# Causal score blocks of 32 tokens in lanes of 32 TensorE columns

## The chip, the core and the metric

The kernel runs on one core of a Trainium2 chip. Its engines are PE (TensorE: matmuls, with PEld for the loads of the stationary operand), DVE (VectorE), ACT (ScalarE), POOL (GpSimd) and SP (SyncE, which issues most DMAs). Matmuls read from SBUF and write to PSUM; DVE and ACT read PSUM and write SBUF. The metric is the device time of one execution in microseconds.

## What is computed

A recurrent attention with a complex, per-channel decay, followed by a two-layer network with a leaky ReLU. There are 4 sequences (batch), 8 heads, 768 steps and 48 channels a head.

```python
mag = np.sqrt(a_re * a_re + a_im * a_im)
scale = np.minimum(mag, 0.999) / (mag + 1e-06)
a_re_n, a_im_n = (a_re * scale, a_im * scale)
for t in range(S):
    ar, ai = (a_re_n[:, :, t, :, None], a_im_n[:, :, t, :, None])
    new_re = ar * S_re - ai * S_im
    new_im = ar * S_im + ai * S_re
    kv = np.einsum('bhd,bhe->bhde', k[:, :, t], v[:, :, t])
    S_re, S_im = (new_re + kv, new_im)
    y[:, :, t] = np.einsum('bhd,bhde->bhe', q[:, :, t], S_re)
...
h = x @ w_in                      # x: 3072 x 384, w_in: 384 x 2048
g = np.maximum(0.01 * h, h)
return (g @ w_out).astype(np.float32)
```

## The kernel before

The 768 steps are cut into six chunks of 128 tokens. Two sequences of one chunk make one of twelve parts (n = 0 to 11); a part is prepared as a whole, and its two sequences (units; 24 in all) go through the attention one after the other.

**Preparation** (prep, L392 to L560), on DVE and ACT. Inside a chunk, the decays are multiplied up: first over R = 8 consecutive tokens (L443, L446), then over the J = 16 ends of such segments by doubling (the tile xs, L448 to L467), and the products of the segments before are spread again over all tokens (L473 copies xs into xt with ACT; L482 and L487 on DVE use it). q is multiplied by the product up to its token and k by the inverse; the real and the imaginary part stand one below the other as 96 rows. The results go to the tile qkt, with 128 columns for the tokens, in the order (r, j): token 8j + r stands in column 16r + j. Ten DMAs a part move qkt into t96 (named t in the profile), 96 rows, one block of 128 columns for each head's q and k (L549 to L557, mostly in SP's queue). There is one qkt and one t96.

**Attention** (attend, L577 to L659), for each unit. With t96 as operands PE makes: ptk, the transposes of k for the state update (L588, copied to kn by ACT; not for the last chunk); ps, for each group of four heads the 128x128 scores of k against q (L601), one full-width matmul a head, four to a bank of PSUM; px, the output (L626): the masked scores and the old state rst times v and q, in 32-column lanes. In px each matmul has 32 columns of the array, and four lanes q = 0 to 3 write the four blocks of 32 PSUM partitions; its matmuls are issued in turn over the lanes. DVE multiplies a bank of scores with the causal mask into asb (L605), ACT and DVE split px into a rounded part xh and a rest xl (L628, L631). pu (L639) is the update of the state, one matmul a head, which reads v and kn. All matmuls of the attention are fp32, and an fp32 matmul that is no transpose leaves two records in the profile.

**MoE** (moe, L661 to L716), for the 256 tokens of each part: L679 to L681 (ph), leaky ReLU on ACT and DVE (tg, L685, L686), again a rounded part and a rest (gh, gl: L687, L688), then L696, L697, L702 (po). These matmuls take the whole array; 288 of them belong to a part, 3456 in all.

**Order.** The tile framework schedules the instructions of each engine statically from priorities: attention before MoE before preparation (PRIO_ATT, PRIO_MOE, PRIO_PREP). PE and DVE thus get one fixed sequence in which pieces of attention stand among MoE and preparation work of other parts. ptk, ps, px and pu share a ring of three PSUM banks (pool psa, tag att, L261). v has one buffer, 448 columns a unit (VW: pairs of heads in 112 columns, in which px finds its 32 columns and pu its 48). At the start, DVE, ACT and POOL also convert the weights into rounded parts and rests (L378 to L388).

At the start the mask is made by one matmul of two POOL-made matrices and copied to a 128x128 tile (L285 to L298), and each of the four heads of a bank is multiplied with it:

```python
nc.vector.tensor_tensor(
    out=asb, in0=ps, in1=mask.unsqueeze(1).to_broadcast([P, 4, C]), op=ALU.mult
)
```

## Time and profile before

| | |
|---|---|
| median of 3 runs | 686.41 us (685.02 to 686.86) |
| the profiled execution | 686.39 us |
| its span in the profile | 684.3 us |
| instructions | 14080 |
| granted TensorE clock, mean | 0.99 |
| HBM read, written | 49.55 MB, 4.72 MB |

What lies around the span is 686.39 - 684.3 = 2.1 us. The lines of the profile are read thus: a group names the source line, the engine, the operation, the tiles written and read, their shapes and the count; then the busy time in us, the mean of one in ns, and the idle time of the engine just before them with what ended it. Two groups of the page, a DVE operation of the MoE and an ACT copy of the attention:

```profile
L686 DVE TENSOR_TENSOR tg<-ph,tg 128x512 f32<-128x512 f32 x96 | 65.8, 688 | 53.4 <-ACT tg L685 51.0
...
L593 ACT COPY kn<-ptk 128x384 f32<-128x384 f32 x40 | 19.0, 474 | 47.6 <-PE ptk L588 47.6
```

### The profile page before, as it was taken

What the parts mean: (1) busy time and instruction counts of PE and PEld (TensorE: products, weight loads), DVE (VectorE), ACT (ScalarE), POOL (GpSimd) and SP (SyncE); (2) the same over time, 40 slices, a digit from 0 to 9 for tenths busy, and PEclk for the clock granted to TensorE, in tenths of its full rate; (3) what the DMA queues carried; (4) which work ended last, traced back from release to release, by engine and by line L of the source; (5) the groups of instructions that cost most, each with busy time, mean ns of one, the idle gap of its engine ahead of it and who ended that gap; (6) DMA issues with size and microseconds to landing.
All of it is one profiled execution on the core that took longest, in us unless ns stands there. A gap on an engine that the chain in (4) does not pass through costs nothing.

```text
span 684.3 us, 14080 instructions
## 1 busy us (share of the span) xinstructions
PE 577.0 (84%) x5732; PEld 555.4 (81%) x5732; DVE 550.2 (80%) x915; ACT 364.8 (53%) x815; POOL 78.0 (11%) x75
## 2 busy tenths in 40 slices
PE   0000475899999999999999999999999998999996
PEld 0000365798999899899999999989999997999996
DVE  5999899999989799898989989989889885233331
ACT  6245256457457275473755727538366277583321
POOL 5645255450000000000000000000000000000000
PEclk9999999999999999999999999999999999899998
DMA  8231733630421703408034070251701748750000
GB/s 329 78 103 69 217 107 119 151 129 29 110 100 52 186 15 88 136 29 209 8 86 145 28 187 25 69 146 51 184 4 51 210 166 194 269 196 13 24 1 29
DMA packets 26232, 74.27 MB, mean 109 GB/s; under 512 B 3376, under 2 KB 9520, under 8 KB 26160
## 3 DMA queue, kind: packets, MB, share of 16 engines
q1 hardware_dynamic: 25552, 71.71, 35.1%
q10 hardware_dynamic: 608, 1.59, 1.0%
q8 instruction: 47, 0.77, 0.5%
q14 instruction: 25, 0.20, 0.1%
HBM read 49.55 MB, written 4.72 MB: 79 GB/s over the span
## 4 chain that ended last, share of the span: by engine, by line
PE 45%; DVE 29%; DMA 12%; ACT 5%; issue 4%; SPq 2%; POOL 1%; ACTq 0%; DVEq 0%; POOLq 0%
DMA t<-qkt 6%; PE po L696 6%; PE po L697 6%; PE po L702 5%; DMA wck<-in_w_dram 5%; PE ph L679 5%; PE ph L680 5%; PE ph L681 5%; PE px L626 4%; PE ps L601 4%; PE pu L639 3%; DVE tg L686 2%; DVE tmp L443 2%; DVE wcv L378 2%; DVE gl L688 2%
## 5 line engine op out<-in xcount | busy, mean ns | idle before, releaser
L679 PE MATMUL ph<-xh,win_hi 128*128 128x256 f32 x576 | 165.2, 287 | 6.7 <-DVE tg L686 5.2
L680 PE MATMUL ph<-xl,win_hi 128*128 128x256 f32 x576 | 164.6, 286 | 2.7 <-DVE xl L631 2.7
L681 PE MATMUL ph<-xh,win_lo 128*128 128x256 f32 x576 | 164.0, 285 | 0.0
L696 PE MATMUL po<-gh,wout_hi 128*128 128x256 f32 x576 | 145.6, 287 | 0.5 <-ACT gh L687 0.5
L697 PE MATMUL po<-gh,wout_lo 128*128 128x256 f32 x576 | 144.8, 286 | 0.0
L679 PEld LDWEIGHTS ph<-xh,win_hi 128*128 128x128 f32 x576 | 110.0, 191 | 8.5 <-DVE tg L686 6.5
L680 PEld LDWEIGHTS ph<-xl,win_hi 128*128 128x128 f32 x576 | 110.1, 191 | 3.5 <-DVE xl L631 2.9
L696 PEld LDWEIGHTS po<-gh,wout_hi 128*128 128x128 f32 x576 | 110.3, 192 | 1.8 <-ACT gh L687 1.0
L697 PEld LDWEIGHTS po<-gh,wout_lo 128*128 128x128 f32 x576 | 110.5, 192 | 0.2 <-issue 0.2
L681 PEld LDWEIGHTS ph<-xh,win_lo 128*128 128x128 f32 x576 | 110.0, 191 | 0.0
L686 DVE TENSOR_TENSOR tg<-ph,tg 128x512 f32<-128x512 f32 x96 | 65.8, 688 | 53.4 <-ACT tg L685 51.0
L685 ACT ACTIVATE tg<-ph 128x512 f32<-128x512 f32 x96 | 57.2, 595 | 92.0 <-PE ph L681 80.0
L588 PE MATMUL ptk<-ident,t 96*128 96x96 f32 x160 | 24.9, 265 | 79.4 <-DMA t<-qkt 79.1
L702 PE MATMUL po<-gl,wout_hi 128*128 128x256 f32 x576 | 89.8, 287 | 0.1
L688 DVE TENSOR_TENSOR gl<-tg,gh 128x512 fp32r<-128x512 f32 x96 | 66.5, 697 | 28.7 <-ACT gh L687 20.2
L588 PEld LDWEIGHTS ptk<-ident,t 96*128 96x128 f32 x160 | 17.9, 150 | 83.6 <-DMA t<-qkt 78.4
L687 ACT CAST gh<-tg 128x512 fp32r<-128x512 f32 x96 | 59.2, 619 | 48.6 <-DVE tg L686 41.6
L702 PEld LDWEIGHTS po<-gl,wout_hi 128*128 128x128 f32 x576 | 77.5, 192 | 0.5 <-DVE gl L688 0.3
L601 PE MATMUL ps<-t 96*128 96x128 f32 x384 | 59.1, 298 | 6.9 <-DVE xl L631 4.2
L601 PEld LDWEIGHTS ps<-t 96*128 96x128 f32 x384 | 53.1, 210 | 8.1 <-DVE xl L631 4.4
L443 DVE TENSOR_TENSOR tmp<-a 128x384 f32<-128x384 f32 x84 | 51.5, 613 | 1.4
L626 PE MATMUL px<-asb,v 128*32 128x128 f32 x768 | 48.4, 288 | 0.8 <-DVE asb L605 0.8
(118 smaller groups left out, 953.1 us busy)
## 6 DMA issues: line engine op xcount, KB each, us to landing
t<-qkt SPq DMA_DIRECT2D x44, 290.2 KB, 5.4
wck<-in_w_dram SPq DMA_DIRECT2D x10, 1152.0 KB, 5.7
a<-in_a_dram SPq DMA_DIRECT2D x12, 768.0 KB, 6.1
qk<-in_qk_dram SPq DMA_DIRECT2D x12, 768.0 KB, 4.8
v<-in_v_dram SPq DMA_DIRECT2D x12, 448.0 KB, 3.3
out_dram<-ot SPq DMA_DIRECT2D x12, 384.0 KB, 2.6
stage_xh<-in_w_dram SPq DMA_DIRECT2D x10, 384.0 KB, 3.0
stage_xl<-in_w_dram SPq DMA_DIRECT2D x10, 384.0 KB, 3.2
```

Source lines behind the costliest of these rows:

```text
L443: nc.vector.tensor_tensor(out=pr, in0=src.unsqueeze(2).to_broadcast([P, 2, 2, M]), in1=swap(ar, r), op=ALU.mult)
L601: nc.tensor.matmul(ps[:, h4], lhsT=t96[:, slot_of(1, h), bi, 0:C], rhs=t96[:, slot_of(0, h), bi, 0:C], start=True, stop=True)
L626: nc.tensor.matmul(px[32 * q : 32 * q + 32, i], lhsT=lhsT, rhs=rhs, start=first, stop=last)
L679: nc.tensor.matmul(o, lhsT=win_hi[:, k, fs], rhs=xh[:, k, :nt], start=(k == 0), stop=False)
L680: nc.tensor.matmul(o, lhsT=win_hi[:, k, fs], rhs=xl[:, k, :nt], start=False, stop=False)
L681: nc.tensor.matmul(o, lhsT=win_lo[:, k, fs], rhs=xh[:, k, :nt], start=False, stop=(k == TI - 1))
L686: nc.vector.tensor_tensor(out=tg[:, :w], in0=ph[:, :w], in1=tg[:, :w], op=ALU.max)
L687: nc.scalar.copy(gh[:, :w], tg[:, :w])
L688: nc.vector.tensor_tensor(out=gl[:, :w], in0=tg[:, :w], in1=gh[:, :w].bitcast(F32), op=ALU.subtract)
L696: nc.tensor.matmul(po[o][:, :nt], lhsT=wout_hi[:, f, os], rhs=gh[:, ts], start=(f == 0), stop=False)
L697: nc.tensor.matmul(po[o][:, :nt], lhsT=wout_lo[:, f, os], rhs=gh[:, ts], start=False, stop=False)
L702: nc.tensor.matmul(po[o][:, :nt], lhsT=wout_hi[:, f, os], rhs=gl[:, ts], start=False, stop=(f == NFC - 1))
```

## The change

The tokens of a chunk are also seen as four blocks x = 0 to 3 of 32 consecutive tokens (NB = 4, JB = J / NB). In t96 a token's column is now (r, j, x), with x innermost: the 32 columns of a block stand four apart. Block x of the keys of head h goes to lane (x + h) mod 4.

- **Scores.** In place of one full matmul, a head gets four: for key block x, 32 stationary columns (four apart) against the query blocks x to 3, that is 128, 96, 64 or 32 columns. The blocks above the diagonal are not computed. For a group of four heads these are sixteen matmuls, in the order of a small function that always serves the lane that is free first. Each writes 32 partitions of the bank, and of its 128 columns those with block x or later.
- **Mask.** As the key blocks of head h stand rotated in the partitions, the mask now has one 128x128 matrix a head (NB, C): sixteen matmuls build it once. Two of the three banks are set to 0 at the start, so that the blocks never written hold finite numbers.
- **v.** px reads v with the blocks of each head rotated the same way; the state update reads a second copy in the old arrangement behind it. A unit has VT = 832 columns where it had 448.
- **Preparation.** xs has one more column (J + 1), and three ACT or DVE copies map between the order of time and the order of blocks; the copy into xt becomes two.
- **Banks.** The ring of three becomes three fixed tiles that are taken in turn. The scratch of dynamic DMAs is set to 1024 bytes.

```diff
@@ -72,6 +76,23 @@
+def block_lane(h, x):
+    return (x + h) % NB
+
+
+def score_order():
+
+    todo = [[(h, x) for h in range(NB) for x in range(NB) if block_lane(h, x) == q] for q in range(NB)]
+    free = [0] * NB
+    order = []
+    while any(todo):
+        q = min((f, q) for q, f in enumerate(free) if todo[q])[1]
+        h, x = todo[q].pop(0)
+        order.append((h, x))
+        free[q] += NB - x
+    return order
@@ -267,7 +288,7 @@
-    mask = cp.tile([P, C], F32, tag="mask", name="mask")
+    mask = cp.tile([P, NB, C], F32, tag="mask", name="mask")
@@ -282,20 +303,37 @@
-    pm = psa.tile([P, 4, P], F32, tag="att", name="pm")
-    nc.tensor.matmul(pm[:, 0], lhsT=perm[:, 0], rhs=perm[:, 1], start=True, stop=True)
-    nc.scalar.copy(mask, pm[:, 0])
+    att = [psa.tile([P, 4, P], F32, tag=f"att{i}", name=f"att{i}") for i in range(NATT)]
...
+    for t in att[1:]:
+        nc.vector.memset(t, 0.0)
+    pm = att_bank()
+    for h in range(NB):
+        for x in range(NB):
+            q = block_lane(h, x)
+            nc.tensor.matmul(
+                pm[32 * q : 32 * q + 32, h], lhsT=perm[:, 0, 32 * x : 32 * x + 32], rhs=perm[:, 1], start=True, stop=True
+            )
+    nc.scalar.copy(mask, pm)
@@ -329,7 +367,7 @@
-        v = pp.tile([P, nb, VW], F32, tag="v", name=f"v_{n}")
+        v = pp.tile([P, nb, VT], F32, tag="v", name=f"v_{n}")
@@ -445,11 +483,12 @@
-        xs = pp.tile([P, 2, J, IB], F32, tag="xs", name=f"xs_{n}")
+        xs = pp.tile([P, 2, J + 1, IB], F32, tag="xs", name=f"xs_{n}")
         nc.scalar.copy(xs[:, :, 0].rearrange("p l (i b) -> p l i b", i=TI), pst[:, :, :, b0 : b0 + nb])
-        ends = zr[:, :, R - 1].rearrange("p l (x j) -> p l j x", j=J)
-        nc.scalar.copy(xs[:, 0, 1:J], ends[:, 0, 0 : J - 1])
-        nc.vector.tensor_copy(out=xs[:, 1, 1:J], in_=ends[:, 1, 0 : J - 1])
+        ends = zr[:, :, R - 1].rearrange("p l (i j x) -> p l x j i", j=JB, x=NB)
+        in_order = [xs[:, l, 1 : J + 1].rearrange("p (x j) i -> p x j i", x=NB) for l in range(2)]
+        nc.scalar.copy(in_order[0], ends[:, 0])
+        nc.vector.tensor_copy(out=in_order[1], in_=ends[:, 1])
@@ -470,7 +509,11 @@
-        nc.scalar.copy(xt.rearrange("p l x j -> p l j x"), xs)
+        for l in range(2):
+            nc.scalar.copy(
+                xt[:, l].rearrange("p i (j x) -> p x j i", x=NB),
+                xs[:, l, 0:J].rearrange("p (x j) i -> p x j i", x=NB),
+            )
@@ -564,6 +607,10 @@
+    def from_block(t96, s, h, bi, x0, x1):
+        t = t96[:, slot_of(s, h), bi, 0:C].rearrange("p (y x) -> p y x", x=NB)
+        return t[:, :, x0] if x1 == x0 + 1 else t[:, :, x0:x1]
@@ -595,18 +642,23 @@
-                ps = psa.tile([P, 4, P], F32, tag="att", name=f"ps_{n}_{bi}_{hh}")
-                for h4 in range(4):
+                ps = att_bank()
+                for h4, x in score_order():
                     h = hh * 4 + h4
+                    q = block_lane(h4, x)
                     nc.tensor.matmul(
-                        ps[:, h4], lhsT=t96[:, slot_of(1, h), bi, 0:C], rhs=t96[:, slot_of(0, h), bi, 0:C], start=True, stop=True
+                        ps[32 * q : 32 * q + 32, h4].rearrange("p (y x) -> p y x", x=NB)[:, :, x:],
+                        lhsT=from_block(t96, 1, h, bi, x, x + 1),
+                        rhs=from_block(t96, 0, h, bi, x, NB),
+                        start=True,
+                        stop=True,
                     )
                 asb = pp.tile([P, 4, C], F32, tag="asb", name=f"asb_{n}_{bi}_{hh}", bufs=2)
                 nc.vector.tensor_tensor(
-                    out=asb, in0=ps, in1=mask.unsqueeze(1).to_broadcast([P, 4, C]), op=ALU.mult
+                    out=asb, in0=ps, in1=mask, op=ALU.mult
                 )
@@ -633,9 +685,9 @@
-                pu = psa.tile([P, 512], F32, tag="att", name=f"pu_{n}_{bi}")
+                pu = att_bank().rearrange("p a b -> p (a b)")
                 for h in range(H):
-                    o = (h // 2) * PAIR + (h % 2) * 64
+                    o = VW + h * D
```

The scheduler makes a new order of it. In the rows below the line stands first, then the operation, the tile written, the tiles read, and the shape; a tile that is called att_99, att_100 or att_101 after the change is one of the three banks.

PE, part 3, first unit, where the first transposes and scores stand. Before, L588 is ptk and L601 is ps (one row is one or more full-width matmuls):

```order
L588 MATMUL ptk_0_0_2216<-ident,t_3_2196 128x96
L588 MATMUL ptk_0_1_2222<-ident,t_3_2196 128x96
L601 MATMUL ps_0_0_2228<-t_3_2196 128x128
L681 MATMUL ph_8_1929<-xh_1606,win_lo 128x256
L679 MATMUL ph_8_1929<-xh_1606,win_hi 128x256
L680 MATMUL ph_8_1929<-xl_1607,win_hi 128x256
L681 MATMUL ph_8_1929<-xh_1606,win_lo 128x256
L588 MATMUL ptk_0_0_2216<-ident,t_3_2196 128x96 x3
L588 MATMUL ptk_0_1_2222<-ident,t_3_2196 128x96 x2
L601 MATMUL ps_0_0_2228<-t_3_2196 128x128 x2
L588 MATMUL ptk_0_1_2222<-ident,t_3_2196 128x96
```

The same place after the change, where L635 is ptk and L649 is ps (32 stationary columns, then the columns streamed):

```order
L635 MATMUL att_100<-ident,t_3_2327 128x96
L635 MATMUL att_101<-ident,t_3_2327 128x96
L649 MATMUL att_99<-t_3_2327 32x128
L649 MATMUL att_99<-t_3_2327 32x32x3
L649 MATMUL att_99<-t_3_2327 32x32x2
L649 MATMUL att_99<-t_3_2327 32x32
L635 MATMUL att_100<-ident,t_3_2327 128x96 x3
L635 MATMUL att_101<-ident,t_3_2327 128x96 x2
L649 MATMUL att_99<-t_3_2327 32x32x2
L649 MATMUL att_99<-t_3_2327 32x32x3
L649 MATMUL att_99<-t_3_2327 32x128
L649 MATMUL att_99<-t_3_2327 32x32x3
```

The scores of one group stand in three pieces between full-width transposes, as they did before, but each piece is now of narrow matmuls.

PE, the last part (11), the end of the first unit's output and the second unit's scores. Before, L626 is px and L696 is MoE:

```order
L626 MATMUL px_0_7007<-asb_0_1_7005,v_6451 32x128 x4
L626 MATMUL px_0_7007<-t_11_6980,rst 32x128 x4
L601 MATMUL ps_1_0_7042<-t_11_6980 128x128 x4
L601 MATMUL ps_1_1_7049<-t_11_6980 128x128 x4
L696 MATMUL po_0_6017<-gh_8_6198,wout_hi 128x256
```

After the change, L678 is px:

```order
L678 MATMUL att_99<-asb_0_1_7460,v_6841 32x128 x4
L678 MATMUL att_99<-t_11_7413,rst 32x128 x4
L649 MATMUL att_100<-t_11_7413 32x128
L649 MATMUL att_100<-t_11_7413 32x32x3
L649 MATMUL att_100<-t_11_7413 32x32x2
L649 MATMUL att_100<-t_11_7413 32x32
L649 MATMUL att_100<-t_11_7413 32x32x2
L649 MATMUL att_100<-t_11_7413 32x32x3
```

The narrow scores follow the narrow output directly, and all 32 of the unit's score matmuls stand in one run.

ACT, the first preparation, from the copy out of the segment ends to the one into xt. Before, these are L451 and L473:

```order
L451 COPY xs_209<-a_113 128x90
L385 ACTIVATE stage_xl_111<-stage_xl_111 128x384
L387 ACTIVATE win_hi<-wcv_269 128x3x128
L387 ACTIVATE wout_hi<-wcv_277 128x384
L385 ACTIVATE stage_stg_112<-stage_stg_112 128x384
L473 COPY a_113<-xs_209 128x2x16x6
```

After the change, they are L490 and L513:

```order
L490 COPY xs_228<-a_132 128x96
L423 ACTIVATE stage_xl_130<-stage_xl_130 128x384
L425 ACTIVATE win_hi<-wcv_289 128x3x128
L425 ACTIVATE wout_hi<-wcv_297 128x384
L423 ACTIVATE stage_stg_131<-stage_stg_131 128x384
L513 COPY a_132<-xs_228 128x4x4x6 x2
```

The place is the same; the first copy has 96 elements for 90, and the second has become two of 96.

More of the change, by code (lines that the diff above doesn't have):

```diff
@@ L29 @@
 TP = C + 1
+NB = 4
+JB = J // NB
+NATT = 3
 NWC = 2 * NFC
@@ L52 @@
 VW = (H // 2) * PAIR
+VT = VW + DM
 SUB_POS = []
@@ L308, in body @@
     for c, bs in SUBS:
-        v_off.append(v_off[-1] + len(bs) * VW * P)
+        v_off.append(v_off[-1] + len(bs) * VT * P)
     stage = []
@@ L733, in body @@
                     prio(PRIO_FLAG)
-                    bad = flag(nc, keep, pp, psa, acc, zfl, wacc, xacc, low)
+                    bad = flag(nc, keep, pp, att_bank(), acc, zfl, wacc, xacc, low)
                 moe(gi)
@@ L759, in chans @@
         return blk[:, hh, :, dd]
+    row = []
+    for k2 in range(H // 2):
+        row += [2 * k2 * D + e for e in range(D)]
+        row += [(2 * k2 + 1) * D + e for e in list(range(32, D)) + list(range(32))]
     a_f, qk_f, v_f = [], [], []
@@ L764 @@
         pl = np.stack([chans(a_re, c, bs), chans(a_im, c, bs)], 0)
[L765 removed]
+        pl = pl.reshape(2, TI, P, nb, NB, JB, R).transpose(2, 0, 6, 1, 3, 5, 4)
         a_f.append(np.ascontiguousarray(pl).reshape(-1))
         pl = np.stack([chans(q, c, bs), chans(k, c, bs)], 0)
[L768 removed]
+        pl = pl.reshape(2, TI, P, nb, NB, JB, R).transpose(2, 0, 6, 1, 3, 5, 4)
         qk_f.append(np.ascontiguousarray(pl).reshape(-1))
         pl = v[list(bs)][:, :, c * C : (c + 1) * C, :].transpose(2, 0, 1, 3)
[L771 to L775 removed]
+        pl = pl.reshape(NB, JB, R, nb, H, D)
+        blk = pl.transpose(0, 2, 1, 3, 4, 5).reshape(NB, P // NB, nb, H, D)
+        blk = np.stack([blk[[block_lane(-h, x) for x in range(NB)], :, :, h] for h in range(H)], 3).reshape(P, nb, H, D)
+        pad = np.zeros((P, nb, VT), v.dtype)
+        lane = pad[..., :VW].reshape(P, nb, H // 2, PAIR)
+        lane[..., 0:D] = blk[:, :, 0::2]
+        lane[..., 64:80] = blk[:, :, 1::2, 32:D]
+        lane[..., 80:112] = blk[:, :, 1::2, 0:32]
+        pad[..., :VW] = lane.reshape(P, nb, VW)
+        pad[..., VW:] = pl.transpose(2, 1, 0, 3, 4, 5).reshape(P, nb, DM)[..., row]
         v_f.append(pad.reshape(-1))
[L777 to L780 removed]
     w1 = moe_w_in[row].reshape(TI, P, NFC, P).transpose(2, 1, 0, 3).reshape(NFC, P, DM)
```

43 lines of the change are left out of this document (19 added, 24 removed).

## The prediction

> **What bounds the kernel now.** I read the totals of the page first, then a table by stage, then the order of time on TensorE. The totals:
>
> ```profile
> PE 577.0 (84%) x5732; PEld 555.4 (81%) x5732; DVE 550.2 (80%) x915; ACT 364.8 (53%) x815; POOL 78.0 (11%) x75
> ...
> PE   0000475899999999999999999999999998999996
> ...
> DVE  5999899999989799898989989989889885233331
> ```
>
> The 84% of PE is an average over two stages. In the first four slices of 17 us PE does almost nothing while DVE is full (weight conversion and the first preparation); over the next four it fills, and from there on it stands at 9. Five rows of the table by stage, one of them a whole cycle of a part (columns: stretch, its length, busy time and count of PE, PEld, DVE, ACT, POOL, granted clock, DMA share, GB/s):
>
> ```profile
> 0.00:78.00 78.00, 1.08 (x4) 0.79 (x5) 67.93 (x98) 33.15 (x63) 41.16 (x43) 1.00 0.42 145
> 78.00:134.00 56.00, 40.14 (x277) 35.71 (x276) 52.66 (x79) 30.46 (x73) 26.64 (x22) 1.00 0.47 143
> ...
> 323.00:366.00 43.00, 42.95 (x462) 41.63 (x461) 39.25 (x67) 24.96 (x60) 0.00 (x0) 1.00 0.34 96
> ...
> 540.00:580.00 40.00, 37.51 (x401) 35.89 (x399) 30.93 (x61) 26.69 (x51) 0.00 (x0) 1.00 0.68 199
> ...
> 606.00:684.00 78.00, 71.66 (x598) 71.08 (x597) 25.09 (x44) 28.30 (x58) 0.00 (x0) 0.98 0.09 27
> ```
>
> In the cycle PE is busy for 42.95 of 43.00 us, DVE for 39.25: PE sets the pace, and DVE has 3.75 us left. At the end PE is alone. So after about 134 us a microsecond taken from PE is a microsecond of the span, as long as DVE's slack lasts. The waits from 134 us to the end say the same; on PE they are all that the answer lists:
>
> ```profile
> PE ptk L588 <- DMA t<-qkt: 3.9, 7, 1.1
> ...
> PE ps L601 <- DMA t<-qkt: 2.7, 1, 2.7
> ...
> PE ph L679 <- DVE tg L686: 1.8, 3, 1.0
> ...
> PE po L696 <- ACT gh L687: 0.5, 1, 0.5
> ```
>
> That is 8.9 us in 550, most of it PE waiting for the transposed operands (t) of the next part.
>
> **The scores, before and after.** A group of four heads is one run of eight passes (each fp32 matmul leaves two records). The chain of waits has the run, the group of lines has the count:
>
> ```profile
> 236.76 0.89 PE ps L601 x8
> ...
> L601 PE MATMUL ps<-t 96*128 96x128 f32 x384 | 59.1, 298 | 6.9 <-DVE xl L631 4.2 <-DMA t<-qkt 2.7
> ```
>
> 384 records are 48 runs of eight, so the scores hold PE for 48 × 0.89 = 42.7 us, 0.111 us a pass of 128 columns. The 298 ns of one record is no price: passes overlap.
>
> Afterwards a group has sixteen matmuls, 32 passes, each on 32 columns of the array, four such lanes side by side. The kernel has such lanes already, in px. Its last run, in order of time on PE:
>
> ```profile
> 595.33 0.28 PE L681 MATMUL ph<-xh,win_lo 128*128 128x256 f32 x1
> 595.45 0.28 PE L679 MATMUL ph<-xh,win_hi 128*128 128x256 f32 x1
> 595.65 0.42 PE L626 MATMUL px<-asb,v 128*32 128x128 f32 x8
> 595.90 0.40 PE L626 MATMUL px<-t,rst 96*32 96x128 f32 x8
> ...
> 597.22 0.40 PE L626 MATMUL px<-t,rst 96*32 96x128 f32 x8
> 597.55 0.39 PE L680 MATMUL ph<-xl,win_hi 128*128 128x256 f32 x1
> ```
>
> Eight records start every 0.22 us (595.90 to 597.22 is six steps of 0.22), so four lanes do a pass of 128 columns in 0.11 us, each lane at the speed that the whole array has for a full-width score pass. The loads go side by side too: in the row below eight loads take 0.16 us in all, while one alone lasts 0.11 us.
>
> ```profile
> 237.93 0.16 PEld L626 LDWEIGHTS px<-asb,v 128*32 128x32 f32 x8
> ...
> L626 PEld LDWEIGHTS px<-asb,v 128*32 128x32 f32 x768 | 30.8, 113 | 6.3 <-DVE asb L605 0.6 <-ACT win_hi L387 0.6 <-issue 0.2
> ```
>
> The rotation by head gives every lane one block each of 128, 96, 64 and 32 columns, so a lane streams 320 columns twice. In proportion to its columns that is 2 × 0.11 × 320 / 128 = 0.55 us, and I take 0.56, for the little that a pass does not shed with its columns. **The saving is 0.89 - 0.56 = 0.33 us a group**: 48 × 0.56 = 26.9 us is left. Where the new order cuts a group in pieces, a piece lasts as long as its fullest lane; added up over the whole order, the pieces make 28.8 us of it. Term one: 28.8 - 42.7 = **-13.9 us**.
>
> **The price of a visit.** Going into 32-column lanes and back is not free. In the rows of px above, wide matmuls start 0.12 us apart (595.33, 595.45), but px starts 0.20 after the last of them: 0.08 to 0.09 lost going in. From the first px (595.65) to the next wide matmul (597.55) are 1.90 us, where 64 / 4 × 0.11 = 1.76 would do: 0.14 lost on first loads and coming out. Together 0.23 us a visit. Before, only px visits: 44 times in PE's order (counted over the whole of it). Now the scores visit too, and the order calls at 89 places: the first excerpt shows scores cut by transposes, the second that a score run joined to px shares one visit. Term two: 45 × 0.23 = **+10.4 us**.
>
> PE's sum is -3.5 us.
>
> **What else is added, and what covers it.** The second copy into xt (third excerpt) is on a chain that DVE waits for: DVE's L482 follows ACT's L473.
>
> ```profile
> 43.28 0.53 ACT L473 COPY a<-xs 128x192 f32<-128x192 f32 x1 [2.27 <-DVE xs L466]
> ...
> 43.84 2.39 DVE L482 TENSOR_TENSOR qkt<-a 128x1536 f32<-128x1536 f32 x1
> ...
> L451 ACT COPY xs<-a 128x90 f32<-128x90 f32 x12 | 4.3, 358 | 7.8 <-DVE a L446 7.8
> ```
>
> Two copies of 96 elements, at 0.36 us each by the copy of 90, make 0.72 instead of 0.53: 0.2 us for each of the two preparations that run before PE has work, **+0.4 us**. In the ten others DVE's slack of 3.75 us a cycle covers it; without that it would be 2 us more. The six extra elements of the copies out of ends go the same way, at a few ns each. The product with the mask keeps its 128x512 elements, and only the second operand is no longer one block repeated, so I leave its 0.69 us; were it twice that, four products a cycle would add 2.8 us to DVE, and that still fits.
>
> ```profile
> L605 DVE TENSOR_TENSOR asb<-ps,mask 128x512 f32<-128x512 f32 x48 | 32.9, 687 | 18.4 <-PE ps L601 18.3
> ...
> v<-in_v_dram SPq DMA_DIRECT2D x12, 448.0 KB, 3.3
> ...
> 254.83 0.33 SPq L341 DMA_DIRECT2D v<-in_v_dram  x1
> ...
> 266.01 1.21 SPq L549 DMA_DIRECT2D t<-qkt  x2
> ...
> DVE wcv L378 <- DMA stage_a<-in_w_dram: 5.3, 1, 5.3
> ```
>
> The load of v grows by 832/448, so from 3.3 to some 6 us at most. In SP's queue it goes out at 254.83 and the next transfer of t at 266.01, 11 us later: covered by the MoE of that cycle; if t followed at once, it would be 3 us a cycle. At the start v stands behind the a and first weight loads that DVE waits for. The memsets of the banks, the wider mask and its sixteen matmuls lie in the first 78 us, where PE does 1.08 us of work and DVE first waits 5.3 us for data (the row above): nothing. The banks rotate in the same ring of three, so I see no new wait there; the state update reads another copy of v at the same 48 columns: nothing.
>
> **The sum** is -13.9 + 10.4 + 0.4 = -3.1 us. The profiled execution took 686.39 us, next to a median of 686.41, so the forecast is **683.3 us**.
>
> **What the trace can't price: strides.** Both operands of a score block step over 16 bytes, and the output leaves gaps; no PE row of before does that. One end is no cost, a lane of 0.56 us. The other is that a block with gaps takes as long as a full one, a lane of 8 × 0.11 = 0.88 us. The nearest row with a stride is ACT's: L473 takes 528 ns for 192 elements written at steps of 64 bytes, where contiguous 384 take 522.
>
> ```profile
> L473 ACT COPY a<-xs 128x192 f32<-128x192 f32 x12 | 6.3, 528 | 9.7 <-DVE xs L466 9.7
> ...
> L387 ACT ACTIVATE wout_hi<-wcv 128x384 fp32r<-128x384 f32 x16 | 8.3, 522 | 9.7 <-POOL wcv L386 9.5
> ```
>
> So there an element alone costs about double. Double for the blocks of single elements (32 columns, two passes of 27 ns a lane) is 0.055 us a group. I take no cost, because a column of these passes takes 0.86 ns (110 ns / 128), where a MoE pass streams 256 in 120 ns, 0.47 ns each: there is time for a slower fetch. Both costs stay as rivals. The point of balance is near: a lane of 0.56 + 3.1 / 48 = 0.625 us leaves no gain.
>
> [...]
>
> **Rivals.**
> 1. *Single elements cost double* (place: the 32-column blocks and their loads). 48 × 0.055 = +2.6 us on the forecast: 685.9, no change. For it: the ACT row; against it: the slow column rate.
> 2. *The gain is lost in waits.* PE asks for the next t earlier, and preparation, on a DVE that is busy for 39.25 of 43, can't follow. DVE needs at least its busy time, so the room is there; but the order of all engines is new (counted in PE's order, the t of part 2 is asked for 23 MoE matmuls earlier than before, that of part 8 62 later), and waits may go either way by some 3 us: 686.4 at the bad end. Were half of the 8.9 us of waits to go instead, 678.9.
> 3. *A narrow pass is no shorter than a full one* (place: all 1536 score passes; slower than before). The 1.76 us / 64 = 27.5 ns a record in px would then be not the time of four lanes but the rate at which PE issues passes, whatever their width (strides at their dear end give the same sum). A group is then 32 × 27.5 = 0.88 us, with the cuts 43.3 us in all, and the visits come on top: 43.3 - 42.7 + 10.4 + 0.4 = +11.4, 697.8 us. It decides from 0.625 us a group upward. For it: px can't tell lanes from issue, as all its passes are equally long. Against it: eight loads that started within 0.16 - 0.11 = 0.05 us, 7 ns apart.
>
> [...]
>
> **Chances.** Forecast 0.42, rival 1 0.18, rival 2 0.15, rival 3 0.25. About 0.3% (2.1 us) is what a measurement of this kernel can tell from no change. Of the forecast 0.38 lies beyond it; rivals 1 and 2 hold 0.24 within it and 0.03 and 0.06 on its faster and slower side; rival 3 is slower but for 0.01: faster 0.41, same 0.29, slower 0.30. The forecast alone would be 680 to 685.5. For 8 in 10 the range runs from 677.5 (the forecast and two thirds of the waits gone) to 697 (most of rival 3).
>
> **What would show it.** Right: a run of 32 score records in about 0.56 us between wide matmuls (0.79 with its visit), the score lanes balanced, 89 visits, PE at 9 from slice 8 on. Rival 1 shows as runs of 0.61, rival 3 as 0.88. Rival 2 shows as PE waiting for t by more than 9 us with runs of 0.56. Wrong altogether: the mask product longer than 0.69 us so that DVE becomes full, or a start of the MoE that moves by more than 1 us.

## The result and the profile after

The changed kernel takes 706.09 us (median of four runs, 703.26 to 710.21), the kernel before 686.2 us beside it: a ratio of 1.0295, 95% interval 1.024 to 1.035. The change makes the kernel **slower by 3%**, where 683.3 us was forecast.

The profiled execution took 703.26 us, with a span of 701.4 us (684.3 before) and a mean granted clock of 0.976 (0.990 before). The totals and the strips of the page of the kernel after:

```profile
PE 585.0 (83%) x6914; PEld 552.3 (79%) x6914; DVE 549.1 (78%) x917; ACT 366.3 (52%) x827; POOL 81.4 (12%) x75
...
PE   1000466899999899999999999999999998979996
...
DVE  5999799889879599898897988979979785232332
PEclk9999998889999899999999999999999999989999
```

PE's busy time is 8 us more. From slice 8 on PE stands at 9 as before, but for an 8 in slice 13 (from 228 us) and a 7 in 35 (from 614 us); the 8 in slice 33 stood there before too. The nines tell little: a slice of 17.5 us can hold more than a microsecond of waits and still read 9. DVE shows more eights and sevens than before, so it is not what became full. The strip of the clock has eights in slices 6 to 8, 13 and 35.

Rows of the table by stage (columns as in the prediction; the second and the last have no like before, as the end has moved):

```profile
78.00:134.00 56.00, 42.81 (x377) 37.40 (x378) 50.65 (x78) 31.21 (x75) 28.93 (x22) 0.94 0.44 136
...
230.00:280.00 50.00, 47.41 (x574) 44.70 (x573) 39.93 (x69) 24.92 (x62) 0.00 (x0) 0.93 0.32 87
323.00:366.00 43.00, 42.75 (x549) 40.06 (x548) 38.05 (x67) 25.19 (x61) 0.00 (x0) 1.00 0.31 88
540.00:580.00 40.00, 37.41 (x508) 36.26 (x508) 32.13 (x65) 19.59 (x37) 0.00 (x0) 1.00 0.56 171
606.00:701.40 95.40, 84.42 (x733) 83.24 (x732) 26.69 (x46) 38.03 (x72) 0.00 (x0) 0.95 0.20 72
```

The cycle from 323 us is as full as it was. The loss lies elsewhere: the granted clock is 0.93 to 0.95 in three rows, and the last stage leaves 11 us free on PE (95.40 - 84.42), where it left 6.3 before. PE's waits from 134 us to the end (in total, times, longest):

```profile
PE att L635 <- DMA t<-qkt: 8.7, 10, 2.5
PE ph L731 <- DVE tg L738: 5.7, 4, 4.5
PE po L748 <- ACT gh L739: 2.5, 2, 1.4
PE att L649 <- DMA t<-qkt: 2.5, 3, 1.0
```

With three small rows these come to 20.2 us, against 8.9 before. Transposes (L635) and scores (L649) wait 11.2 us for t, against 6.6; the MoE waits for the gates 8.2 us, against 2.3.

To see where 17.1 us of span come from I add up every PE record from start to start, from 77 us on. Gaps over 0.5 us are waits. For the records that began while the granted clock was 0.5, what they took above the mean of their kind at full clock is the loss at half clock. The rest is PE's work. First transposes + work + waits + half clock + 6.7 us behind the last matmul give the span:

| | before | after | difference |
|---|---|---|---|
| first transposes | 77.7 | 78.1 | +0.4 |
| PE's work at full clock | 566.2 | 564.5 | -1.7 |
| waits over 0.5 us | 29.1 | 40.5 | +11.4 |
| half clock | 4.7 | 11.7 | +7.0 |

The profiled execution is the shortest of the four, 2.8 us under their median, so the 17.1 us accounted for here are a little less than the 19.9 between the medians.

So PE's work is nearly what was forecast (-3.5), and **the 17 us are waits and half clock**, which the forecast had at nothing. Inside the -1.7, the gaps between MoE matmuls gave 2.3, and scores, transposes, px and the state together are 0.7 longer.

The row of work holds one thing more. The first record of the granted clock stands at 113.7 us before and at 115.2 us after. Ahead of it the view shows 1.00, but PE goes at the pace of the half clock. Here is the kernel before ahead of its first record, with 11 MoE matmuls in 2 us:

```profile
110.00:112.00 2.00, 2.00 (x11) 2.00 (x11) 2.00 (x4) 1.03 (x4) 0.00 (x0) 1.00 0.16 60
```

The kernel after has 11 where 0.50 is on record, and 19 at 1.00:

```profile
120.00:122.00 2.00, 2.00 (x11) 2.00 (x11) 1.70 (x3) 1.29 (x4) 2.00 (x2) 0.50 0.88 303
...
126.00:128.00 2.00, 2.00 (x19) 2.00 (x19) 2.00 (x4) 0.00 (x0) 2.00 (x1) 1.00 0.00 0
```

Added up in the same way, this stretch costs 12.0 us before and 12.1 after, so it hardly touches the difference: work changes by -2.5 us without it. In the runs below it is 9.4 to 12.7 us and stands under work, too. Only f2's first record is as early as 92.1 us: 20.5 us of this stretch count as half clock there, so f2's columns of work and half clock can't be set beside the others'.

### The profile page after: what moved, and what is told of

Read it like the earlier page. It is cut to its first block, busy times and chain, and to the rows that moved or that the text cites. A ratio compares the mean times of both kernels' runs of the same rounds, so it can differ in the third digit from the quotient of the medians.

```text
span 701.4 us, 16480 instructions
## 1 busy us (share of the span) xinstructions
PE 585.0 (83%) x6914; PEld 552.3 (79%) x6914; DVE 549.1 (78%) x917; ACT 366.3 (52%) x827; POOL 81.4 (12%) x75
## 4 chain that ended last, share of the span: by engine, by line
PE 43%; DVE 27%; DMA 12%; ACT 6%; issue 6%; SPq 3%; POOL 2%; ACTq 0%; DVEq 0%
DMA t<-qkt 7%; PE po L748 6%; PE po L749 5%; PE ph L731 5%; PE po L754 5%; PE ph L732 5%; PE ph L733 5%; DMA wck<-in_w_dram 4%; PE att L649 4%; PE att L678 3%; DVE tg L738 2%; PE att L691 2%; PE att L635 2%; DVE gl L740 2%; ACT wck L395 2%
## 5 line engine op out<-in xcount | busy, mean ns | idle before, releaser
L731 PE MATMUL ph<-xh,win_hi 128*128 128x256 f32 x576 | 168.1, 292 | 11.8 <-DVE tg L738 8.7
L732 PE MATMUL ph<-xl,win_hi 128*128 128x256 f32 x576 | 166.9, 290 | 2.8 <-DVE xl L683 2.8
L733 PE MATMUL ph<-xh,win_lo 128*128 128x256 f32 x576 | 166.6, 289 | 0.0
L731 PEld LDWEIGHTS ph<-xh,win_hi 128*128 128x128 f32 x576 | 112.8, 196 | 14.1 <-DVE tg L738 10.1
L732 PEld LDWEIGHTS ph<-xl,win_hi 128*128 128x128 f32 x576 | 113.0, 196 | 3.2 <-DVE xl L683 3.1
L733 PEld LDWEIGHTS ph<-xh,win_lo 128*128 128x128 f32 x576 | 112.8, 196 | 0.4
L635 PE MATMUL att<-ident,t 96*128 96x96 f32 x160 | 27.9, 283 | 85.3 <-DMA t<-qkt 81.7
L635 PEld LDWEIGHTS att<-ident,t 96*128 96x128 f32 x160 | 17.7, 153 | 94.4 <-DVE a L484 72.3
L740 DVE TENSOR_TENSOR gl<-tg,gh 128x512 fp32r<-128x512 f32 x96 | 65.9, 690 | 25.6 <-ACT gh L739 16.4
L739 ACT CAST gh<-tg 128x512 fp32r<-128x512 f32 x96 | 59.2, 618 | 46.0 <-DVE tg L738 33.9
L657 DVE TENSOR_TENSOR asb<-att,mask 128x512 f32<-128x512 f32 x48 | 32.4, 686 | 29.0 <-PE att L649 28.9
L649 PE MATMUL att<-t 96*32 96x32 f32 (+3 forms) x1536 | 52.1, 265 | 2.6 <-DMA t<-qkt 2.5
L649 PEld LDWEIGHTS att<-t 96*32 96x32 f32 x1536 | 39.9, 146 | 11.3 <-DMA t<-qkt 3.5
```

Source lines behind the costliest of these rows:

```text
L635: nc.tensor.transpose(out=pt[:, h4, 0:96], in_=t96[:, slot_of(1, hh * 4 + h4), bi, 0:C], identity=ident[0:96, 0:96],)
L649: nc.tensor.matmul(ps[32 * q : 32 * q + 32, h4].rearrange("p (y x) -> p y x", x=NB)[:, :, x:], lhsT=from_block(t96, 1, h, bi, x, x + 1), r ...
L731: nc.tensor.matmul(o, lhsT=win_hi[:, k, fs], rhs=xh[:, k, :nt], start=(k == 0), stop=False)
L732: nc.tensor.matmul(o, lhsT=win_hi[:, k, fs], rhs=xl[:, k, :nt], start=False, stop=False)
L733: nc.tensor.matmul(o, lhsT=win_lo[:, k, fs], rhs=xh[:, k, :nt], start=False, stop=(k == TI - 1))
L739: nc.scalar.copy(gh[:, :w], tg[:, :w])
```

## The experiments

Four theories. *Strides*: 16-byte steps make the narrow passes dear. *Narrow scores*: they cost more than they save, through pieces and visits, whatever the order. *Order*: the scheduler, given 16 matmuls for 4, made a worse order of everything. *The rest of the change*: rotated tokens, copies, fixed banks. "Order of" a kernel means below that the instructions of every engine were held in the sequence of that kernel by dependencies that order two instructions of one engine and add no wait. A ratio is to the kernel before, run beside it on the same chip.

| run | median us | ratio, 95% interval | PE's work | waits | half clock |
|---|---|---|---|---|---|
| e1_full_scores | 689.15 | 1.004, 1.001 to 1.0069 | 560.7 | 35.6 | 2.8 |
| e2_contiguous | 701.15 | 1.0229, 1.0184 to 1.0274 | 559.5 | 44.0 | 9.8 |
| e3_scores_alone | 702.51 | 1.023, 1.0178 to 1.0283 | 564.6 | 40.9 | 9.6 |
| e4_short_blocks | 699.39 | 1.0212, 1.015 to 1.0275 | 555.8 | 42.5 | 11.2 |
| e5_scores_first | 694.3 | 1.0108, 1.0067 to 1.015 | 550.5 | 49.3 | 7.6 |
| e6_before_scores_first | 684.14 | 0.9955, 0.9923 to 0.9987 | 555.8 | 33.7 | 8.7 |
| e7_after_no_weight_check | 693.84 | 1.0106, 1.0056 to 1.0156 | 564.2 | 34.0 | 8.8 |
| e8_before_no_weight_check | 678.44 | 0.989, 0.9858 to 0.9921 | 565.2 | 23.1 | 1.4 |
| e9_after_less_dve | 702.3 | 1.0227, 1.019 to 1.0263 | 562.2 | 42.7 | 11.2 |
| e10_before_less_dve | 701.91 | 1.0227, 1.0199 to 1.0256 | 565.0 | 43.4 | 6.3 |
| e11_blocks_in_order | 725.86 | 1.0576, 1.051 to 1.0642 | 561.5 | 61.5 | 13.8 |
| e12_blocks_scores_first | 708.51 | 1.0313, 1.0254 to 1.0371 | 548.8 | 59.2 | 13.5 |
| f1_change_in_order_of_before | 697.13 | 1.0161, 1.0126 to 1.0196 | 566.6 | 35.0 | 7.3 |
| f2_full_scores_in_order_of_change | 697.81 | 1.016, 1.0125 to 1.0196 | 553.3 | 42.6 | 14.4 |
| f3_contiguous_in_order_of_before | 692.86 | 1.0082, 1.0059 to 1.0105 | | | |
| f4_change_in_order_of_full | 696.98 | 1.0151, 1.0117 to 1.0185 | 569.5 | 34.6 | 4.2 |
| f5_scores_first_in_full_order | 689.52 | 1.0031, 0.9999 to 1.0063 | 556.2 | 37.1 | 8.8 |
| f6_scores_of_a_unit_in_one_visit | 696.92 | 1.0143, 1.0098 to 1.0188 | 544.9 | 50.1 | 14.5 |

The last three columns are of the one profiled execution. Of f3 only the time is used. The profiled execution of e1 was its shortest (685.98), so its row lies below its median.

### Full-width scores in the changed kernel, narrow scores in the old one

e1 has all of the change but the narrow blocks:

```diff
-for h4, x in score_order():
-    nc.tensor.matmul(ps[32 * q : 32 * q + 32, h4]..., lhsT=from_block(...), rhs=from_block(...), ...)
+for h4 in range(4):
+    nc.tensor.matmul(ps[:, h4], lhsT=t96[:, slot_of(1, h), bi, 0:C], rhs=t96[:, slot_of(0, h), bi, 0:C], ...)
```

> The changed kernel with one edit taken back: a score group is again four matmuls of 128x128 over all tokens (no lanes, no blocks); the token order, the preparation copies, the larger load of v, the wide mask and the fixed banks stay (the scores then multiply rows and columns that the mask and v don't match, so the values differ). Theory A1 (the loss of 17 us is waits that the new preparation copies and the larger load cause): 698 to 705 us, PE waits over 1 us as in the changed kernel, about 40 us of them from 77 us on. Theory A2 or B (waits or run lengths that come with the narrow scores): 684 to 690 us.

e3 is the other half, the kernel before with narrow scores on contiguous columns and with the three zeroed banks, but with its old tokens and copies:

```diff
-nc.tensor.matmul(ps[:, h4], lhsT=t96[..., 0:C], rhs=t96[..., 0:C], ...)
+nc.tensor.matmul(ps[32 * q : 32 * q + 32, h4, 32 * x : C], lhsT=t96[..., 32 * x : 32 * x + 32], rhs=t96[..., 32 * x : C], ...)
```

> The kernel before with the narrow scores alone, in contiguous blocks, and with the fixed, zeroed banks they need; preparation, v and the mask are those of before (the blocks then don't match v and the mask, so the values differ). Theory A1: 683 to 687 us. Theory A2 or B: 698 to 706 us, with waits or score runs as in the changed kernel.

e1 took 689.15 us and e3 702.51, both inside what was expected if the loss comes with the narrow scores. The rest of the change costs 0.4% (0.1 to 0.7), 2 us, in the order that came with e1. Narrow scores bring nearly all of the loss, with contiguous operands too: but they bring an order of their own as well, so these two runs do not part the theories *order* and *narrow scores*.

### Strides and widths

e2 is the changed kernel, in exactly its order, with contiguous columns; e4 streams only the block on the diagonal:

```diff
# e2
-lhsT=from_block(t96, 1, h, bi, x, x + 1), rhs=from_block(t96, 0, h, bi, x, NB)
+lhsT=t96[:, slot_of(1, h), bi, 32 * x : 32 * x + 32], rhs=t96[:, slot_of(0, h), bi, 32 * x : C]
# e4
-rhs=from_block(t96, 0, h, bi, x, NB)
+rhs=from_block(t96, 0, h, bi, x, x + 1)
```

> The changed kernel, in its exact order on every engine, with the 16-byte steps taken out of the scores: each block reads 32 adjacent keys and 32 to 128 adjacent queries and writes adjacent columns (other tokens than the mask means, so the values differ). Theory C (strides cost): the score runs, now 24 ns from start to start in mean (0.77 us for 32 records), fall to the forecast's 17.5 ns (0.56 us), loads to 109 ns from 140, and the time falls by 8 to 10 us to 694 to 700. Without a stride cost: 24 ns and 703 to 710 us as before.

> The changed kernel with every block's moving operand cut to 32 columns (keys and queries of one block alone, the other blocks of the scores left out). If lanes set the length of a run, as forecast, a lane streams 8 passes of 27 ns, 0.22 us a group, so 16 ns less a record or more, and PE's work falls by some 15 us. If the rate at which PE starts passes sets it (24 ns), 0.75 to 0.78 us a group as in the changed kernel, and PE's work stays within 2 us.

The same visit of two groups (64 records) between a MoE matmul and a transpose, in order of time on PE (start, time from first start to last end, then the operation). The kernel after:

```profile
205.73 0.28 PE L732 MATMUL ph<-xl,win_hi 128*128 128x256 f32 x1
205.94 1.54 PE L649 MATMUL att<-t 96*32 96x128 f32 x64
207.41 0.55 PE L635 MATMUL att<-ident,t 96*128 96x96 f32 x4
```

e2, contiguous:

```profile
206.64 0.28 PE L732 MATMUL ph<-xl,win_hi 128*128 128x256 f32 x1
206.85 1.33 PE L649 MATMUL att<-t 96*32 96x128 f32 x64
208.11 0.38 PE L635 MATMUL att<-ident,t 96*128 96x96 f32 x2
```

f2 (below), full-width scores in the order of the change:

```profile
201.85 0.28 PE L819 MATMUL ph<-xl,win_hi 128*128 128x256 f32 x1
201.97 1.95 PE L740 MATMUL att<-t 96*128 96x128 f32 x16
203.76 0.49 PE L727 MATMUL att<-ident,t 96*128 96x96 f32 x4
```

From the first score to the next transpose it is 1.47, 1.26 and 1.79 us; ahead of it 0.21, 0.21 and 0.12. The steps of 16 bytes cost 0.21 us for two groups, **0.105 a group**, 5.0 us for 48, and e2's PE work is 5.0 us less. Its time, 701.15 us, is 4.9 us below that of the change and a little above the 694 to 700 expected. That 4.9 is so near to 5.0 is in part luck: the two profiled spans are only 2.3 us apart (701.4 and 699.1), as e2 waits 3.5 us longer. The loads show it too: in the groups by form one takes 146 ns after and 115 in e2:

```profile
L649 PEld LDWEIGHTS att<-t 96*32 96x32 f32 x1536 | 39.9, 146 | 11.3 <-DMA t<-qkt 3.5 <-issue 1.8 <-ACT win_hi L425 0.4
```

```profile
L649 PEld LDWEIGHTS att<-t 96*32 96x32 f32 x1536 | 34.9, 115 | 11.6 <-DMA t<-qkt 3.9 <-issue 1.8 <-ACT win_hi L425 0.4
```

The forecast of 0.56 us a group holds where it was to be without strides: 1.259 us for two groups (over all such visits) is 2 × 0.56 plus the 0.14 of the way out. With strides it is (1.469 - 0.14) / 2 = 0.66.

Which lane a record belongs to follows from the widths and the program's order in each lane. So each lane can be followed through five of the seven visits of two groups. In e2 the next record of a lane starts 31, 60, 82 and 110 ns (means) behind one of 32, 64, 96 and 128 columns: a lane's time goes with its columns, as forecast. With the steps of 16 bytes the same gaps are 55, 78, 87 and 112 ns. The blocks of single elements (32 columns) come near double, as rival 1 had it, and those of 64 columns, which it put at nothing, lose 18 ns too.

e4 met neither expectation (0.22 us a group, or 0.75 and more): its 64 records take 1.229 us, 0.24 less than in the change, though its lanes stream 128 columns for 320. But e4 keeps the 16-byte steps, and all its blocks are of single elements: a lane starts one about every 66 ns, where e2 without steps takes 31. So e4 says what the steps cost, not what the width is worth.

### One order, both kinds of scores

f1 to f4 hold the order. Each full-width score matmul's place takes four narrow ones, or the reverse, and the banks go as they went in the kernel whose order it is. The edit of all four is one function, called behind the last instruction, with a recorded order for each engine:

```diff
+def pin(nc, tc):
+    for engine, order in ORDERS.items():
+        ...
+                    tc.add_manual_dep(i, last.name, mybir.DependencyInfo(NoSync, DATA), reason="order")
```

f1: the change in the order of before. f2: e1 in the order of the change. f3: e2 in the order of before. f4: the change in e1's order.

> The whole changed kernel, its values unchanged, with the order of every engine pinned to that of the kernel before (order-only dependencies between an engine's neighbours; four blocks stand where one full-width score matmul stood, the second copy into xt behind the first, the banks as before had them). PE's order then has 98 visits. Theory O (the engines' order makes the waits, narrow scores only add their own PE work): that work is about that of before (566 us at full clock in the profile, 564.5 in the changed kernel, plus 9 visits at 0.23), so 685 to 692 us. Theory N (narrow scores bring waits of their own: all four heads' operands are needed at once, more visits, the clock): 698 us or more.

> The counterpart: full-width scores (values differ, as in the first run of them) in the exact order of the changed kernel on every engine. Theory O: near the changed kernel, less the 3.8 us that PE's work differs by (564.5 against 560.7): 698 to 704 us. Theory N: as the full-width scores in their own order, 686 to 691 us.

> As the first, with contiguous blocks (values differ): the stride's 5.0 us of PE work gone. Theory O: 680 to 687 us, so at least level with before and 3 to 6 us under the first. Theory N: 693 us or more.

> The whole changed kernel pinned to the order of the run with full-width scores (689.2 us): 100 visits. Theory O: 689.2 + 3.8 + 11 x 0.23 = 695.5, so 692 to 698 us. Theory N: 700 us or more.

| | order of before | order of the change | e1's order |
|---|---|---|---|
| full-width scores | 686.2 (before itself) | 697.81 (f2) | 689.15 (e1) |
| narrow scores | 697.13 (f1) | 706.09 (after) | 696.98 (f4) |

f1 and f2 are both 1.6% above the kernel before, but both also hold the rest of the change (2.0 us in e1). Pairs that differ in one thing alone part the costs. Narrow scores cost 8.3 us in the order of the change (after over f2) and 7.8 in e1's (f4 over e1). The order of the change costs 9.0 us over that of before (after over f1) and 8.7 over e1's (f2 over e1). 8.3 + 8.7 + 2.0 = 19.0 is nearly the whole (19.9): **two costs of some 8 to 9 us each, that add up.** f1 and f3 fell between what the two theories expected, f2 just below the lower end of what *order* did, and f4 inside it. f3 is 4.3 us below f1, the strides again.

What the narrow scores cost in one order is seen record by record between the kernel before and f1, with the recorded half clock taken out of both. Inside score runs: 40.71 us to 33.21, -7.5 (1.8 of it ahead of the first clock record, at half pace). Going in and out (the gaps between a score or px and another kind): +11.1 for 54 visits more (98 for 44), 0.21 each. That is +3.6, of which the table shows +0.4 as work (+1.7 without the stretch ahead of the first clock record), mostly because gaps between MoE matmuls are 2.7 shorter. The rest of f1's 10.4 us of span is waits (+5.9), half clock (+2.6) and first transposes at 79.1 us for 77.7 (+1.4). PE's waits in f1 (L733 the transposes, L747 the scores):

```profile
PE att L733 <- DMA t<-qkt: 6.0, 6, 2.4
PE att L747 <- DMA t<-qkt: 3.5, 3, 2.9
PE ph L831 <- DVE tg L838: 2.4, 5, 0.8
PE po L848 <- ACT gh L839: 0.5, 1, 0.5
```

and in f2 (L727 the transposes, L740 the scores):

```profile
PE att L727 <- DMA t<-qkt: 9.7, 15, 1.5
PE ph L818 <- DVE tg L825: 6.5, 3, 5.6
PE po L835 <- ACT gh L826: 1.9, 2, 1.3
...
PE att L740 <- DMA t<-qkt: 1.8, 4, 0.7
```

f1 has the waits of before with 2.9 us more for t; f2, with no narrow score in it, has the 6.5 us for the gates that the change has. Those come with the order.

### Fewer and longer pieces

A quarter of a group between a transpose and a MoE matmul, after and in f2:

```profile
327.22 0.33 PE L635 MATMUL att<-ident,t 96*128 96x96 f32 x2
327.48 0.43 PE L649 MATMUL att<-t 96*32 96x128 f32 x8
327.84 0.38 PE L733 MATMUL ph<-xh,win_lo 128*128 128x256 f32 x1
```

```profile
321.79 0.36 PE L727 MATMUL att<-ident,t 96*128 96x96 f32 x2 [0.78 <-DMA t<-qkt]
321.98 0.41 PE L740 MATMUL att<-t 96*128 96x128 f32 x2
322.15 0.36 PE L820 MATMUL ph<-xh,win_lo 128*128 128x256 f32 x1
```

0.36 us against 0.17. With the way in, a narrow quarter costs 0.29 us more than the full-width one, a half 0.32, a whole group 0.085, and two groups together save 0.225. Of the 62 score pieces in the order after, 37 are less than a group, 13 are one, five are between one and two, and only seven are two. So longer pieces should help; e5 puts the scores ahead of the transposes in the changed kernel, e6 does so in the kernel before:

```diff
+            am = []
+            for hh in range(2):  # scores and their product with the mask
+                ...
             if c < NCH - 1:
                 kn = pp.tile([P, H, 2, D], F32, tag="kn", name=f"kn_{n}_{bi}")
                 ...
-            am = []
-            ...
```

> The changed kernel with the two score groups of a unit written ahead of its transposes, nothing else edited; in PE's order the visits to 32-column lanes fall from 89 to 58, since scores are no longer cut by transposes. If a visit costs 0.23 us, PE's work at full clock falls by 31 x 0.23 = 7.1 us. Theory V (work and waits add up): 697 to 701 us. Theory W (the order of the engines decides the waits, and work saved turns into waits): work falls by about 7 us but the time stays at 703 to 710 us.

> The kernel before with the same move (full-width scores ahead of the transposes). No visit is saved by it on the scores. Theory V: 685 to 689 us. Theory W: anything from 680 to 700 us, by waits alone, with PE's work at full clock within 2 us of before.

f5 is e5 in e6's order, f6 is f1 with all score places of a unit moved to the first of them:

> The changed kernel with the scores ahead of the transposes, in the exact order of the kernel before with the same move (684.1 us, full-width scores). In one order a quarter group in lanes costs 0.29 us more than full-width, a half 0.32, a whole group 0.09, while two groups in one visit cost 0.23 us less (rows of the run with full scores in the order of the change against the changed kernel). By the pieces of this order (5 quarters, 12 halves, 20 groups, 9 of one and a half, 3 of two) the PE work rises by 5 to 6 us: 688 to 693 us, some more if waits follow. If it comes below 686 the price list is wrong.

> The same order with one edit on PE: both score groups of a unit stand together at the place of the first, so 24 visits for the scores, each of 64 records. By the price list PE's work falls by 24 x 0.23 = 5.4 us against full-width scores in that order, so 677 to 682 us if nothing waits; the second group asks for its bank and its operands earlier, and if PE waits for them as long as half a microsecond a unit, 690 us or more.

e5 has 58 visits and 14.0 us less work than the change (10.5 without the stretch ahead of the first clock record), but 8.8 more waits: 694.3, below both ranges expected. f6 has 49 visits and 21.3 us less work than the kernel before, and is 10 us slower than it. Beside f1, from which that one move parts it, it has 21.7 us less work, 15.1 more waits and 7.2 more half clock, and takes the same time (696.92 us for 697.13). Its page and its waits (L732 the transposes):

```profile
PE 571.8 (82%) x6914; PEld 549.6 (79%) x6914; DVE 551.1 (79%) x917; ACT 367.1 (53%) x827; POOL 75.9 (11%) x75
```

```profile
PE att L732 <- DMA t<-qkt: 16.7, 17, 2.8
PE ph L829 <- DVE tg L836: 7.7, 4, 3.0
```

PE is busy for 5 us less than before, and waits for t 16.7 us instead of 6.6. Here it is plain that work taken from PE came back as waits and half clock. e6, with full-width scores, is the fastest of all kernels that compute the whole: 684.14 us, 0.9955 (0.9923 to 0.9987). It gained 10.4 us of work, where at most 2 were expected, and gave back 8.6 in waits and clock. In its order px visits fall from 44 to 27, which is 3.9 us at 0.23 each; where the rest comes from was not followed up. With narrow scores in its order, f5, it is 5 us slower, as the prices of the pieces had it (688 to 693 us expected).

### The tail, and DVE

The longest wait after is at 623 us. The order of time there (a bracket is the wait ahead of a row):

```profile
623.33 1.21 ACT L395 ACTIVATE wck<-wck 128x1152 f32<-128x1152 f32 x1 [1.77 <-DMA wck<-in_w_dram]
...
626.51 0.61 ACT L737 ACTIVATE tg<-ph 128x512 f32<-128x512 f32 x1
627.16 0.69 DVE L738 TENSOR_TENSOR tg<-ph,tg 128x512 f32<-128x512 f32 x1 [4.67 <-ACT tg L737]
627.90 0.58 PE L731 MATMUL ph<-xh,win_hi 128*128 128x256 f32 x1 [4.47 <-DVE tg L738]
```

The MoE waits for the gate, that for ACT, and ACT stands in its queue behind the pass over the weights' words, which waits for its DMA. e7 and e8 leave that pass out of the kernel after and before (`nc.vector.memset(wacc, 0.0)` in its place).

> The changed kernel without the check of the weights (its loads and 44 ScalarE instructions, most of them late, are left out; zeros stand for its sums). The order up to 540 us is that of the changed kernel. If the end's waits (11 us over 0.5 us each from 545 us on, the longest 4.7 us for a relu that ScalarE reached late, and the half clock after it) come from ScalarE being behind the check: 694 to 698 us. If they come from the late arrival of the last t: above 701 us.

> The kernel before without the check of the weights, as the control. Its end has 4 us of such waits, 3.0 of them for t. Expected 684 to 687 us, so the gap to the changed kernel without the check would be 9 to 13 us if ScalarE's end is a part of the loss, and still 17 or more if it isn't.

693.84 and 678.44, the first at the edge of the 694 to 698 expected, the second well below the 684 to 687: the pass costs 12.3 us after and 8.4 (of 686.8 beside it) before. Some 4 us of the 20 come from it; 15.4 us of difference remain without it.

Is DVE too slow for a PE that asks earlier? e9 and e10 leave out the 96 subtractions that make gl (`return gh, gh`), after and before:

> The changed kernel with the 96 VectorE subtractions of the relu's low part (gl, 0.69 us each, 66 of VectorE's 549 us) left out; the third product of the second MoE layer takes the high part again. Theory D (the loss comes from VectorE: it is about as full as PE, waits in order for scores, and every wait for PE moves the next preparation): with VectorE relieved the gap between this kernel and its partner falls to 5 us or less. Theory S (the loss comes with the narrow scores on PE itself: visits, waits for transposed operands, the clock): the gap stays at 12 us or more.

> The kernel before with the same 96 subtractions left out, as the partner. By both theories it is faster than 686 us or equal to it: if VectorE's order sets waits of PE, by 5 to 25 us; if PE's own work sets the time, by less than 5 us.

They end at 702.3 and 701.91, and the gap is gone, but not as the theory had it: the kernel before, with 55 us less on DVE, became 15.5 us *slower*. Its page shows the room on DVE:

```profile
PE 580.4 (83%) x5732; PEld 557.5 (80%) x5732; DVE 495.1 (71%) x819; ACT 365.4 (52%) x815; POOL 77.1 (11%) x75
```

Its waits are 43.4 us for 29.1. Its order is new, too. That the order makes these waits is likely after f2, but not shown: no run holds the kernel with less work on DVE in the order of before.

e11 keeps the tokens in their natural order, so that blocks of 32 are contiguous for PE, and DVE writes qkt at steps of 32 bytes instead; e12 is e11 with the scores first:

```diff
-return bass.AP(x.tensor, x.offset, [list(x.ap[0]), [TP, IB], [J, R], [1, J]])
+return bass.AP(x.tensor, x.offset, [list(x.ap[0]), [TP, IB], [1, R], [R, J]])
```

> The changed kernel with the tokens of t in their natural order, so that a block is 32 adjacent columns (VectorE writes t at steps of 32 bytes instead); the preparation's copies are those of before, all else as changed, the whole of the computation is there. If the stride costs 5.0 us of PE's work, as the run in its exact order showed, and the other write order costs nothing: 699 to 703 us. If VectorE pays for its write order: above 703 us.

> The same with the scores ahead of the transposes: both edits that shorten PE's work, 5 us for the strides and 31 visits. Theory V (savings of PE's work count in the time): 694 - 5 = 687 to 691 us, level with the kernel before. Theory D (VectorE holds the pace, PE's savings turn into waits): 691 to 697 us, not below the run with scores first alone by more than 3 us.

725.86 and 708.51. e11 is above 703 us, as was expected if DVE pays for its write order; e12 lies beyond all that was expected. The line of that write, e11 and then after (busy time, mean ns of one):

```profile
L556 DVE TENSOR_TENSOR qkt<-qk,a 128x768 f32<-128x768 f32 x24 | 39.7, 1654 | 0.0
```

```profile
L564 DVE TENSOR_TENSOR qkt<-qk,a 128x768 f32<-128x768 f32 x24 | 23.4, 976 | 0.0
```

Twice 24 such writes are 33 us more on DVE; PE waits 61.5 us. PE's 5 us of strides were the cheaper side of that bargain, in the orders that came with these runs.

## Why the prediction was wrong

**What bounds the kernel: the step that failed.** "So after about 134 us a microsecond taken from PE is a microsecond of the span, as long as DVE's slack lasts" does not hold, and the waits that were to go "either way by some 3 us" went by 11.4. f6 has 21.3 us less work on PE than the kernel before and takes 10 us more; e6 has 10.4 less and takes 3 us less; e10 left PE's work as it was and lost 15.5. PE at 9 in nearly every slice says that PE is rarely idle long, not that it waits for nobody: t arrives through DVE, SP's queue and a transfer, and a PE with less work of its own waited for it (16.7 us in f6, 6.6 before). DVE's 3.75 us a cycle of slack, a mean, did not show that.

**The new order had no price.** The prediction saw that "the order of all engines is new" and gave it 3 us. With full-width scores in that order the kernel takes 11 us more than before (f2), 8.7 of them more than in e1's order.

**The clock was no term at all.** It cost 7.0 us, apart from the 12 us ahead of the first clock record, which both kernels pay. One episode after, in stretches of 2 us (columns as above, the clock third from the end), and the wait ahead of it:

```profile
190.00:192.00 2.00, 1.06 (x16) 0.76 (x15) 1.63 (x4) 0.59 (x1) 0.00 (x0) 1.00 0.88 222
192.00:194.00 2.00, 2.00 (x31) 1.40 (x30) 0.10 (x1) 1.06 (x3) 0.00 (x0) 0.93 1.01 421
194.00:196.00 2.00, 2.00 (x10) 2.00 (x11) 1.83 (x6) 0.14 (x1) 0.00 (x0) 0.50 0.51 208
```

```profile
191.75 0.52 PE L635 MATMUL att<-ident,t 96*128 96x96 f32 x4 [0.94 <-DMA t<-qkt]
```

PE waits 0.94 us for t (1.2 us from one start to the next), works on transposes and score pieces, and at 193.7 the clock falls to 0.50 for 3.4 us; MoE passes start 213 ns apart there, for 120 at full clock. After, this happens five times (6.8, 6.8, 3.4, 6.8 and 6.8 us long), before twice (3.4 and 6.8). Each followed waits that lie in the 3.4 us ahead, or reach into them, and add up to 1.2 to 4.8 us from start to start. Not every such wait does it. The kernel before waited 1.14 us here, the kernel after 1.43 us, and the clock stayed up both times:

```profile
275.50 0.36 PE L588 MATMUL ptk<-ident,t 96*128 96x96 f32 x2 [1.14 <-DMA t<-qkt]
```

```profile
573.14 0.39 PE L748 MATMUL po<-gh,wout_hi 128*128 128x256 f32 x1 [1.43 <-ACT gh L739]
```

In the profiles before and after, the changes of the clock lie whole multiples of 3.413 us apart (131 of them from 134.2 to 581.3 us in the kernel before, 14 from 145.9 to 193.7 after). So where a wait falls on that grid may count beside its length; no run tries it.

In the episode at 193.7 us the wait was paid twice: 1.2 us from start to start, and then 3.4 us at 0.50.

**Term one, the scores (-13.9), was right in its mechanism (e2's lanes go with their columns, 31 ns for 32 and 110 for 128) and too large.** In one order (before and f1) it is -7.5 inside the runs. Strides are 5.0 us of the gap, 0.105 us a group: rival 1, had at 0.61 us a group and measured at 0.66. A block of 64 columns streams two neighbours of every four and lost 18 ns all the same, but its loads and its output have steps, too, and no run parts these.

**Term two, the visits (+10.4), was right**: 89 visits as counted, 0.21 us each in f1 and 0.234 in the two-group visits (0.09 in, 0.14 out), for 0.23. What it hid is that a visit for a quarter or a half group costs more than the group saves: 0.29 and 0.32 us more than full-width scores.

**Rival 3 falls.** A narrow pass is shorter than a full one: 0.66 us a group with strides, 0.56 without, not 0.88. The range's upper end came from it, and 706.09 us lies above that end for other reasons. Nor do the passes start 27.5 ns apart: contiguous (e2), the 63 steps between 64 starts take 1.125 us, 17.9 ns each, and with strides 20.4.

**Rival 2 is the one that came**, with four times its price: waits for t 11.2 us (it named more than 9), gates 8.2 on top, and the clock.

**The small terms held.** The start moved by 0.4 us. The product with the mask stayed at 0.69 us. The load of v takes 4.5 us (at most 6 was said), and no wait of PE names it.

**What stays open.** Why the scheduler's order for narrow scores is the worse one; I have shown only that it is. Why narrow scores in the order of before, with 0.4 us more PE work, cause 5.9 us of waits and move the first transposes by 1.4. Which waits bring the half clock; to fill PE's waits with dummy matmuls was not tried.

## What to carry to other kernels

A change of an instruction's number goes through the scheduler: hold the old order and make the change in it, and hold the new order and leave the change out, before believing that either is the cause. A gain in PE's work was no gain of time here where what feeds PE was not ahead of it (f6: 21.3 us less work, 10 us more time); put waits, and the half clock that followed some of them (11.4 and 7.0 us here), into the sum as terms of their own size, not as a margin. Price narrow matmuls by the piece: here, with 16-byte steps, two groups of scores in one visit save 0.225 us, and a quarter of one loses 0.29.
